# A Fourier mixing layer and an MLP mixer on one core: a rebuilt kernel with 64x64 array tiles, resident filters and no output transposes

## The chip, the cores and the metric

One core of a Trainium2 chip. The time is the device time of one execution in microseconds (us). Runs of the undisturbed state are called "fast". A "ratio" is always the mean time of one kernel's fast runs over that of the kernel before in the same rounds, so it is not quite the ratio of the medians that stand beside it. The profile is one traced execution; its span is about 2 us shorter than the measured time.

Names of engines: PE is TensorE's matmuls, PEld its weight loads, DVE is VectorE, ACT ScalarE, POOL GpSimd, SP SyncE. A *group* or *block* below is 512 tokens of the MLP. A *pair* is two of the eight batches; both kernels work on four pairs. PSUM is where the matmuls leave their sums; an *eviction* is the copy of a PSUM tile into a tile that later steps read.

## The reference, cut to what matters

```python
def _attn_ref(x, filt_r, filt_i):                 # x: (8, 3136, 256)
    X = np.fft.rfft(x, axis=1)
    Y = X * (filt_r + 1j * filt_i)[None]          # one filter per frequency and channel
    return np.fft.irfft(Y, n=x.shape[1], axis=1)

def _moe_ref(x, U, V, w_ch1, w_ch2):              # U: (3136, 32), V: (32, 3136)
    xt = x.transpose(0, 2, 1)
    h = xt @ U @ V                                # low-rank mixing over the sequence
    u = x + h.transpose(0, 2, 1)
    ch = np.maximum(u @ w_ch1, 0.0) @ w_ch2       # 256 -> 1024 -> 256
    return u + ch
```

Both kernels take the length 3136 = 64 x 49 apart: a transform over 64 (first stage), a store and a reload that turn the data, a transform over 49 with the filter and its inverse (here called *mid*), a store and a reload, and the inverse transform over 64 (last stage). Then the low-rank term, then the MLP. Everything between is float16, sums are float32.

## The kernel before: the parts that the argument touches

```python
    def stage_f1c(bp):          # first stage: 64 rows, 128 columns (real and imaginary of 64 frequencies)
        ...
                    nc.tensor.matmul(pf1[:, 0:nn * DM], w64c[64 * i:64 * i + 64, :],
                                     x16[64 * i:64 * i + 64, n2 * DM:(n2 + nn) * DM], ...)
    def stage_mid(bp):          # per frequency: two matmuls, two multiplies, two matmuls, ACT copy
        ...                     # filters come again for each pair: fag, fbg
    def stage_i2(bp):           # last stage: 66 rows, 64 columns, writes y16
        ...
    def stage_lr(bp):           # low rank, after the whole of y16 is there
        for r in range(N2):     # 49
            for i in range(2):
                nc.tensor.matmul(ph1[i][32 * i:32 * i + 32, :],           # 64 rows, 32 columns
                                 usb[64 * i:64 * i + 64, r * RANK:(r + 1) * RANK],
                                 y16[64 * i:64 * i + 64, r * DM:(r + 1) * DM], ...)
        ...
        for r in range(N2):
            pg = ppf.tile([128, DM], F32, tag="m", bufs=3)
            for i in range(2):
                nc.tensor.matmul(pg[64 * i:64 * i + 64, :],               # 32 rows, 64 columns
                                 vsb[32 * i:32 * i + 32, r * N1:(r + 1) * N1],
                                 h1sb[32 * i:32 * i + 32, :], start=True, stop=True)
            nc.vector.tensor_add(y16[:, r * DM:(r + 1) * DM], y16[:, r * DM:(r + 1) * DM], pg[:, :])
    def stage_mlp(bp):
        def mm2_part(prev):
            ...
            for eh in range(2):
                pc = ppf.tile([128, 512], F32, tag="m", bufs=3)
                for t in range(8):
                    nc.tensor.matmul(pc[:, 0:nr * 128],                   # weights stationary
                                     w2sb[:, t * DM + eh * 128:t * DM + eh * 128 + 128],
                                     h16[t][:, 0:nr * 128], start=(t == 0), stop=(t == 7))
                cht = sb.tile([128, 512], F16, tag="cht", bufs=2)
                nc.scalar.copy(cht[:, 0:nr * 128], pc[:, 0:nr * 128])
                for rr in range(nr):                                      # back to tokens in rows
                    nc.tensor.transpose(pq[:, rr * DM + eh * 128:rr * DM + eh * 128 + 128],
                                        cht[:, rr * 128:(rr + 1) * 128], idn[:, 0:128])
        ...
```

The stages are Python generators, woven together: while one pair is in its last stage, low rank and MLP, the next pair is in mid and the one after that in its first stage.

Of the kernel before, what the change touches and what calls it, by code (L numbers as in the profile page):

```python
# [12 lines left out]


SEQ = 3136
N1, N2 = 64, 49
NK1 = 33
DM = 256
RANK = 32  # L20
NF = SEQ // 2 + 1
NG = [3] * 11
NGP = 7


def _consts():
    W64 = np.exp(-2j * np.pi * np.outer(np.arange(N1), np.arange(N1)) / N1)
    W49 = np.exp(-2j * np.pi * np.outer(np.arange(N2), np.arange(N2)) / N2)
    tw = np.exp(-2j * np.pi * np.outer(np.arange(N1), np.arange(N2)) / SEQ)
    w64c = np.concatenate([W64.real.T, W64.imag.T], axis=1)  # L30
    perm = np.arange(N2)
    perm[25:] = 73 - perm[25:]
    tc1 = np.zeros((NK1, N2, 98))
    tc2 = np.zeros((NK1, N2, 98))
    for a in range(NK1):
        Wp = W49 * tw[a][None, :]
        tc1[a, :, :N2] = Wp.real.T[:, perm]
        tc1[a, :, N2:] = Wp.imag.T[:, perm]
        tc2[a, :, :N2] = -Wp.imag.T[:, perm]
        tc2[a, :, N2:] = Wp.real.T[:, perm]  # L40
    ctw = np.exp(2j * np.pi * np.outer(np.arange(NK1), np.arange(N2)) / SEQ)
    g1 = np.zeros((NK1, 98, 98))
    g2 = np.zeros((NK1, 98, 98))
    for a in range(NK1):
        T1 = (W49.conj() * ctw[a][:, None]) / SEQ
        tr, ti = T1.real.T[perm, :], T1.imag.T[perm, :]
        g1[a][:N2, :N2] = tr
        g1[a][:N2, N2:] = ti
        g1[a][N2:, :N2] = -tr
        g1[a][N2:, N2:] = -ti  # L50
        g2[a][:N2, :N2] = -ti
        g2[a][:N2, N2:] = tr
        g2[a][N2:, :N2] = -ti
        g2[a][N2:, N2:] = tr
    g1[:, 49 + 25:98, :] *= -1.0
    g2[:, 25:49, :] *= -1.0
    w = np.exp(2j * np.pi * np.outer(np.arange(N1), np.arange(NK1)) / N1)
    cr = w.real.copy()
    ci = -w.imag.copy()
    cr[:, 1:32] *= 2.0  # L60
    ci[:, 1:32] *= 2.0
    s2 = np.zeros((66, 64))
    s2[0::2, :] = cr.T
    s2[1::2, :] = ci.T
    f16 = np.float16
    return (w64c.astype(f16), tc1.astype(f16), tc2.astype(f16),
            g1.astype(f16), g2.astype(f16), s2.astype(f16))
# [3 lines left out]
def kernel(  # L71
# [12 lines left out]
    B = x.shape[0]  # L84
    npair = B // 2
    w64_np, tc1_np, tc2_np, g1_np, g2_np, s2_np = _consts()

    w64_d = nc.inline_tensor(np.ascontiguousarray(w64_np), name="w64c")
    tcc_d = nc.inline_tensor(np.ascontiguousarray(
        np.stack([tc1_np, tc2_np], 1).reshape(NK1 * 2, N2, 98)), name="tcc")  # L90
    g12_d = nc.inline_tensor(np.ascontiguousarray(
        np.stack([g1_np, g2_np], 1).reshape(NK1 * 2, 98, 98)), name="g12")
    s2_d = nc.inline_tensor(np.ascontiguousarray(s2_np), name="s2")

    ct1 = nc.dram_tensor("ct1", (B, NK1, N2, 2, DM), F16, kind="Internal")
    ct2 = nc.dram_tensor("ct2", (B, N2, NK1, 2, DM), F16, kind="Internal")

    cst = ctx.enter_context(tc.tile_pool(name="cst", bufs=1))
    sb = ctx.enter_context(tc.tile_pool(name="sb", bufs=1))
    ppf = ctx.enter_context(tc.tile_pool(name="ppf", bufs=2, space=bass.MemoryType.PSUM))  # L100

    ftd = nc.dram_tensor("ftd", (2, 98, NK1, DM), F16, kind="Internal")
    ftdv = ftd.ap()
    for t, part, src in ((0, 0, filt_r), (0, 49, filt_i), (1, 0, filt_i), (1, 49, filt_r)):
        nc.gpsimd.dma_start(
            ftdv[t, part:part + 25],
            bass.AP(tensor=src.tensor, offset=0,
                    ap=[[64 * DM, 25], [DM, NK1], [1, DM]]))
        nc.gpsimd.dma_start(
            ftdv[t, part + 25:part + 49],  # L110
            bass.AP(tensor=src.tensor, offset=64 * DM,
                    ap=[[64 * DM, 24], [-DM, NK1], [1, DM]]))

    w64c = cst.tile([128, 128], F16)
    nc.sync.dma_start(w64c[0:64, :], w64_d.ap())
    nc.sync.dma_start(w64c[64:128, :], w64_d.ap())
    tcc = cst.tile([N2, NK1 * 2 * 98], F16)
    nc.sync.dma_start(tcc, tcc_d.ap().rearrange("a n m -> n a m"))
    g12 = cst.tile([98, NK1 * 2 * 98], F16)
    nc.sync.dma_start(g12, g12_d.ap().rearrange("a j m -> j a m"))  # L120
    s2t = cst.tile([66, 64], F16)
    nc.sync.dma_start(s2t, s2_d.ap())
    idn = cst.tile([128, 128], F16)
    make_identity(nc, idn)
# [4 lines left out]
    usb = cst.tile([128, N2 * RANK], F16)  # L129
    uap = moe_U.rearrange("(q r) p -> q r p", q=N1)  # L130
    nc.gpsimd.dma_start(usb[0:64, :], uap)
    nc.gpsimd.dma_start(usb[64:128, :], uap)
    vsb = cst.tile([64, N2 * N1], F16)
    vnat = sb.tile([RANK, SEQ], F32, tag="x16")
    nc.sync.dma_start(vnat, moe_V)
    nc.vector.tensor_copy(vsb[0:32, :], vnat.rearrange("p (q r) -> p r q", q=N1))  # L136
    nc.sync.dma_start(vsb[32:64, :], vsb[0:32, :])

    st = [dict() for _ in range(npair)]

    def stage_x(bp):
        x16 = sb.tile([128, N2 * DM], F16, tag="x16")
        st[bp]["x16"] = x16
        for i, b in enumerate((2 * bp, 2 * bp + 1)):
            nc.gpsimd.dma_start(x16[64 * i:64 * i + 64, :],
                                x[b].rearrange("(q r) d -> q (r d)", q=N1))

    def stage_f1c(bp):
        bA, bB = 2 * bp, 2 * bp + 1
        x16 = st[bp]["x16"]  # L150
        ne = [0]
        for g0 in range(0, N2, NGP):
            gn = min(NGP, N2 - g0)
            asbg = sb.tile([128, 2 * NGP * DM], F16, tag="asbg", bufs=2)
            for i in range(2):
                for n2 in range(g0, g0 + gn, 2):
                    nn = min(2, g0 + gn - n2)
                    pf1 = ppf.tile([128, 512], F32, tag="a", bufs=3)
                    nc.tensor.matmul(pf1[:, 0:nn * DM],  # L159
                                     w64c[64 * i:64 * i + 64, :],  # L160
                                     x16[64 * i:64 * i + 64, n2 * DM:(n2 + nn) * DM],
                                     start=True, stop=True)
                    dst = asbg[:, (i * NGP + n2 - g0) * DM:(i * NGP + n2 - g0 + nn) * DM]
                    if ne[0] % 2:
                        nc.scalar.copy(dst, pf1[:, 0:nn * DM])  # L165
                    else:
                        nc.vector.tensor_copy(dst, pf1[:, 0:nn * DM])
                    ne[0] += 1
            for i, b in enumerate((bA, bB)):
                for c in range(2):  # L170
                    nc.gpsimd.dma_start(  # L171
                        ct1.ap()[b, :, g0:g0 + gn, c, :],
                        asbg[64 * c:64 * c + NK1,
                             i * NGP * DM:(i * NGP + gn) * DM].rearrange(
                                 "k (n d) -> k n d", d=DM))
            yield

    def load_a2g(bp, gi):
        kgn = NG[gi]
        kg0 = sum(NG[:gi])  # L180
        a2g = sb.tile([N2, 2 * NG[0] * 2 * DM], F16, tag="a2g", bufs=2)
        for i, b in enumerate((2 * bp, 2 * bp + 1)):
            nc.sync.dma_start(
                a2g[:, i * NG[0] * 512:i * NG[0] * 512 + kgn * 512],
                ct1.ap()[b, kg0:kg0 + kgn].rearrange("k n c d -> n k (c d)"))
        return a2g

    def load_ftab(kg0, kgn):
        fag = sb.tile([98, kgn * DM], F16, tag="fag", bufs=2)
        fbg = sb.tile([98, kgn * DM], F16, tag="fbg", bufs=2)  # L190
        nc.sync.dma_start(fag.rearrange("p (k d) -> p k d", k=kgn),
                          ftdv[0, :, kg0:kg0 + kgn, :])
        nc.sync.dma_start(fbg.rearrange("p (k d) -> p k d", k=kgn),
                          ftdv[1, :, kg0:kg0 + kgn, :])
        return fag, fbg

    def stage_mid(bp):
        bA, bB = 2 * bp, 2 * bp + 1
        a2g_next, ft_next = st[bp].pop("pre", None) or (load_a2g(bp, 0), load_ftab(0, NG[0]))
        pend = []  # L200
        done_groups = []

        def do_i1(items):
            for (k1, kl, uv, esb) in items:
                pi1 = ppf.tile([128, 512], F32, tag="q", bufs=2)
                for l in range(2):
                    nc.tensor.matmul(pi1[0:98, :],  # L207
# [5 lines left out]
        for gi in range(len(NG)):  # L213
# [27 lines left out]
            if len(pend) > 1:  # L241
                do_i1(pend.pop(0))
# [26 lines left out]
    def stage_i2(bp):  # L269
# [4 lines left out]
        for cl in range(0, N2 * DM, 1024):  # L274
# [20 lines left out]
            if nchip % 3 == 0:  # L295
                yield
# [186 lines left out]
```

## Time and profile before

| | before |
|---|---|
| median of the first 3 runs | 1033.84 us (1032.45 to 1037.25) |
| span of the profile | 1029.0 us |
| PE, DVE, ACT busy | 857, 499, 397 us |
| time at half clock | about 455 us (0 to 353, 500 to 551, 712 to 746, 879 to 896) |
| 512 tokens in the stretch with the MLP alone | 9.8 us |

From the page of the kernel before: span and busy times, the lines of part 2 for PE and its granted clock (40 equal slices, tenths), and the chain that ended last (share by engine, then by engine, tile and line).

```profile
span 1029.0 us, 11955 instructions
...
PE 857.2 (83%) x4184; PEld 338.0 (33%) x4184; DVE 498.5 (48%) x833; ACT 396.8 (39%) x769; POOL 278.7 (27%) x418
...
PE   0017098786999999999999999998999988988884
PEclk9999999999999999999757999998599999699997
...
PE 66%; ACT 6%; DMA 4%; DVE 3%; POOL 2%; issue 2%; ACTq 0%; POOLq 0%; SPq 0%; DVEq 0%
PE pc L337 17%; PE phh L376 16%; PE py L287 4%; PE pg L317 3%; PE pq L344 3%; ACT cht L342 3%; PE pt L362 2%; DMA ct<-esb 2%; DMA x_972<-in_x_dram 1%; POOL ct L256 1%; PE ph_1252 L304 1%; ACT asbg L165 1%; ACT esb L211 1%; DVE y_3234 L321 1%; DVE y_5483 L321 1%
```

The chain is two thirds PE, and well over half of that share are the matmuls of the MLP (L337, L376), the input transposes (L362) and the output transposes (L344). The clock line shows three dips (at some 500 to 550, 720 to 745 and 875 to 900 us), a fourth in the last slice, where the program ends, and otherwise nines. That line is treacherous here: the clock records of this trace begin at 353 us, and where nothing is recorded a 9 is printed.

From the timeline of the kernel before (start, duration, engine, line, operation; "x2" are merged neighbours, and a merged duration runs from the first start to the last end):

```profile
start us, us, engine line op out<-in xcount [idle before <-releaser]
439.70 0.38 PE L337 MATMUL pc<-h_5_2726,w2sb 128*128 128x512 f16 x1
439.92 0.38 PE L337 MATMUL pc<-h_6_2727,w2sb 128*128 128x512 f16 x1
...
522.26 0.66 PE L207 MATMUL pi_4017<-uv,g_77 98*98 98x512 f16 x1 [0.18 <-DVE uv L237]
522.86 1.08 PE L230 MATMUL pf_3999<-a2g,tcc 49*98 49x512 f16 x2
...
900.79 0.38 PE L337 MATMUL pc<-h_7_7994,w2sb 128*128 128x512 f16 x1
901.85 0.40 PE L344 MATMUL pq<-idn,cht 128*128 128x128 f16 x4 [0.68 <-ACT cht L342]
902.08 0.38 PE L337 MATMUL pc<-h_0_7987,w2sb 128*128 128x512 f16 x1
```

At 439 us 512-wide matmuls start 216 ns apart. At 523 us one takes 0.66 us and two take 1.08 us together, so they start some 430 ns apart: half the rate. Up to 353 us, too, 512-wide matmuls that follow each other start 380 to 460 ns apart, most of them 427 or more, and none near 216 (but for pairs that run at once on two tiles). So the clock is halved for the first 353 us also. The last three lines are one block's round trip: the second MLP matmul is issued for the last time at 900.79, the transposes of its output come 1.06 us later (0.68 us of it PE sits idle, released by the ACT copy).

### The profile page before, as it was taken

Reading aid. Unit: us, or ns where it says so; the run is one execution under the profiler, and the core shown is the slowest. Engines: PE = TensorE matmul, PEld = TensorE weight load, DVE = VectorE, ACT = ScalarE, POOL = GpSimd, SP = SyncE. Lnnn points to the kernel's source line nnn. Section 1 sums busy time; section 2 is a strip of 40 time slices with the busy share of each in tenths; the row PEclk is TensorE's granted clock in tenths of the full one; section 3 lists DMA queues with packets and bytes.
Section 4 is the critical chain, followed back from the end, with each engine's and each line's share of the span. In section 5 each row is a group of like instructions: output and inputs, shape, how many; then the busy total and the mean of one; then the engine's idle time right before and its main releaser. Section 6 shows DMA issues by size and latency. Waiting matters only on the chain.

```text
span 1029.0 us, 11955 instructions
## 1 busy us (share of the span) xinstructions
PE 857.2 (83%) x4184; PEld 338.0 (33%) x4184; DVE 498.5 (48%) x833; ACT 396.8 (39%) x769; POOL 278.7 (27%) x418
## 2 busy tenths in 40 slices
PE   0017098786999999999999999998999988988884
PEld 0001022221233344344433444454344434434332
DVE  0026066552357575546675754566744332733322
ACT  0004042232221356666114555652265543245442
POOL 3006044634223254214323420245210111001101
PEclk9999999999999999999757999998599999699997
DMA  9763744674328355433323554354143212012121
GB/s 164 124 154 111 158 131 131 165 202 137 99 71 199 102 166 157 126 92 96 109 76 113 156 174 121 82 141 151 36 114 107 64 43 66 1 41 62 49 55 47
DMA packets 93501, 113.07 MB, mean 110 GB/s; under 512 B 27092, under 2 KB 78716, under 8 KB 92796
## 3 DMA queue, kind: packets, MB, share of 16 engines
q0 software_dynamic: 32960, 70.00, 27.8%
q1 hardware_dynamic: 60480, 42.30, 14.4%
q8 instruction: 33, 0.54, 0.2%
q14 instruction: 28, 0.23, 0.1%
HBM read 77.30 MB, written 55.49 MB: 129 GB/s over the span
## 4 chain that ended last, share of the span: by engine, by line
PE 66%; ACT 6%; DMA 4%; DVE 3%; POOL 2%; issue 2%; ACTq 0%; POOLq 0%; SPq 0%; DVEq 0%
PE pc L337 17%; PE phh L376 16%; PE py L287 4%; PE pg L317 3%; PE pq L344 3%; ACT cht L342 3%; PE pt L362 2%; DMA ct<-esb 2%; DMA x_972<-in_x_dram 1%; POOL ct L256 1%; PE ph_1252 L304 1%; ACT asbg L165 1%; ACT esb L211 1%; DVE y_3234 L321 1%; DVE y_5483 L321 1%
## 5 line engine op out<-in xcount | busy, mean ns | idle before, releaser
L256 POOL DMA_DIRECT2D ct<-esb x160 | 119.3, 750 | 177.4 <-ACT esb L211 166.3
L350 POOL DMA_DIRECT2D out_dram<-och x104 | 56.3, 546 | 347.7 <-DVE och L347 325.3
L171 POOL DMA_DIRECT2D ct<-asbg x112 | 77.9, 699 | 160.8 <-ACT asbg L165 146.9
L342 ACT CAST cht<-pc 128x512 f16<-128x512 f32 (+1 forms) x104 | 58.3, 561 | 148.6 <-PE pc L337 148.6
L376 PEld LDWEIGHTS <-w1sb 128*128 128x128 f16 x832 | 76.1, 100 | 105.0 <-issue 42.3
L337 PEld LDWEIGHTS <-w2sb 128*128 128x128 f16 x832 | 76.7, 98 | 75.8 <-issue 4.4
L159 PEld LDWEIGHTS <-w64c 64*128 64x128 f16 x224 | 19.5, 108 | 148.1 <-issue 135.9
L317 PE MATMUL pg<-h1sb,vsb 32*64 32x256 f16 x392 | 64.2, 387 | 1.9 <-ACT h1sb L312 0.3
L230 PEld LDWEIGHTS <-tcc 49*98 49x98 f16 x264 | 32.5, 154 | 92.0 <-issue 88.3
L207 PEld LDWEIGHTS <-g_77 98*98 98x98 f16 x264 | 33.5, 151 | 73.0 <-issue 61.9
L344 PE MATMUL pq<-idn,cht 128*128 128x128 f16 x392 | 39.9, 222 | 20.5 <-ACT cht L342 19.4
L159 PE MATMUL pf_102<-x_98,w64c 64*128 64x512 f16 x1 | 0.6, 582 | 67.0 <-DMA x_98<-in_x_dram 67.0
L344 PEld LDWEIGHTS <-cht 128*128 128x128 f16 x392 | 23.1, 97 | 58.4 <-ACT cht L342 56.6
L317 PEld LDWEIGHTS <-vsb 32*64 32x64 f16 x392 | 25.9, 126 | 49.5 <-issue 47.4
L136 DVE CAST vsb<-vnat 32x3136 f16<-32x3136 f32 x1 | 5.7, 5697 | 50.2 <-DMA vnat<-in_moe_V_dram 50.2
L287 PEld LDWEIGHTS <-s2t 66*64 66x64 f16 x200 | 12.3, 113 | 46.9 <-issue 46.0
L165 ACT CAST asbg<-pf_105 128x512 f16<-128x512 f32 x1 | 0.6, 585 | 66.0 <-PE pf_105 L159 66.0
L304 PEld LDWEIGHTS <-usb 64*32 64x32 f16 x392 | 19.2, 96 | 19.6 <-issue 16.1
L293 DVE CAST y_982<-py 128x512 f16<-128x512 f32 (+1 forms) x13 | 8.2, 665 | 33.1 <-PE py L287 33.1
L321 DVE TENSOR_TENSOR y_982<-y_982,pg 128x256 f16<-128x256 f16 x49 | 17.3, 413 | 11.2 <-PE pg L317 11.2
L321 DVE TENSOR_TENSOR y_5483<-y_5483,pg 128x256 f16<-128x256 f16 x49 | 17.1, 412 | 10.1 <-PE pg L317 10.1
L230 PE MATMUL pf_322<-a2g,tcc 49*98 49x512 f16 x2 | 1.1, 628 | 24.6 <-DMA a2g<-ct 24.6
(2306 smaller groups left out, 2054.6 us busy)
## 6 DMA issues: line engine op xcount, KB each, us to landing
out_dram<-och POOLq DMA_DIRECT2D x96, 256.0 KB, 3.7
ct<-asbg POOLq DMA_DIRECT2D x112, 115.5 KB, 2.7
a2g<-ct SPq DMA_DIRECT2D x88, 147.0 KB
ct<-esb POOLq DMA_DIRECT2D x176, 73.5 KB, 3.4
fag<-ftd SPq DMA_DIRECT2D x44, 147.0 KB
fbg<-ftd SPq DMA_DIRECT2D x44, 147.0 KB
x_98<-in_x_dram POOLq DMA_DIRECT2D x2, 1568.0 KB, 14.6
x_311<-in_x_dram POOLq DMA_DIRECT2D x2, 1568.0 KB, 17.5
```

Source lines behind the costliest of these rows:

```text
L171: nc.gpsimd.dma_start(ct1.ap()[b, :, g0:g0 + gn, c, :], asbg[64 * c:64 * c + NK1, i * NGP * DM:(i * NGP + gn) * DM].rearrange("k (n d) -> ...
L207: nc.tensor.matmul(pi1[0:98, :], g12[:, (k1 * 2 + l) * 98:(k1 * 2 + l + 1) * 98], uv[:, l * 512:(l + 1) * 512], start=(l == 0), stop=(l == 1))
L230: nc.tensor.matmul(pf2[0:98, :], tcc[:, (k1 * 2 + l) * 98:(k1 * 2 + l + 1) * 98], rhs, start=(l == 0), stop=(l == 1))
L256: nc.gpsimd.dma_start(ct2.ap()[b, :, kh0:kh0 + khn, c, :], src)
L287: nc.tensor.matmul(py[64 * i:64 * i + 64, 0:w], s2t[:, :], e2c[i][:, sub:sub + w], start=True, stop=True, tile_position=(0, 64 * i))
L317: nc.tensor.matmul(pg[64 * i:64 * i + 64, :], vsb[32 * i:32 * i + 32, r * N1:(r + 1) * N1], h1sb[32 * i:32 * i + 32, :], start=True, stop= ...
L321: nc.vector.tensor_add(y16[:, r * DM:(r + 1) * DM], y16[:, r * DM:(r + 1) * DM], pg[:, :])
L337: nc.tensor.matmul(pc[:, 0:nr * 128], w2sb[:, t * DM + eh * 128:t * DM + eh * 128 + 128], h16[t][:, 0:nr * 128], start=(t == 0), stop=(t = ...
L342: nc.scalar.copy(cht[:, 0:nr * 128], pc[:, 0:nr * 128])
L344: nc.tensor.transpose(pq[:, rr * DM + eh * 128:rr * DM + eh * 128 + 128], cht[:, rr * 128:(rr + 1) * 128], idn[:, 0:128])
L350: nc.gpsimd.dma_start(out[b].rearrange("(q r) d -> q r d", q=N1)[:, r0:r0 + nr, :], och[64 * i:64 * i + 64, 0:nr * DM])
L376: nc.tensor.matmul(phh[:, 0:nr * 128], w1sb[:, dh * 1024 + t * 128:dh * 1024 + (t + 1) * 128], ut[dh][:, 0:nr * 128], start=(dh == 0), sto ...
```

## The change: its intent, and its core

The kernel was rewritten. Its intents were: smaller array tiles where operands have 64 rows and 64 columns, so that four matmuls run at once; the filter table read once and kept; the low-rank product U computed on the spectrum (before the last FFT stage) and V accumulated into the PSUM tile of that stage, so that neither a separate pass nor an addition is left; the MLP's second matmul with the hidden tokens as stationary operand, so that its output has tokens in its rows and needs no transpose; and the last FFT stage done per group of 512 tokens, just ahead of the MLP that uses it. The diff is almost the whole file; its core, with cuts marked "...":

```diff
 # first FFT stage
-    w64c: [128, 128], one 64-row tile, 128 output columns, 56 matmuls per pair
+    wf1: [128, 64]; 48 matmuls per pair on 64x64 tiles, four at once
+                for i in range(nb):
+                    for h in range(2):
+                        nc.tensor.matmul(pf[64 * h:64 * h + 64, i, :],
+                            wf1[64 * i:64 * i + 64, :],
+                            u.x[c][64 * i:64 * i + 64, h, 2 * half:2 * half + 2, :], ...)
 # mid: filters resident, one matmul instead of two, one multiply instead of two
-        fag, fbg = load_ftab(...)                # again for each pair
+    fab = cst.tile([98, NK, 2, DM], F16)         # once
+            pz = ps.tile([128, 512], F32, tag="z", bufs=2, name="pz")
+            nc.tensor.matmul(pz[0:98, 0:bd], tf2[:, k * 98:(k + 1) * 98],
+                             a2[slot // 4][:, slot % 4, :], start=True, stop=True)
+            nc.vector.tensor_mul(uv..., zin, fin)            # 98 x 1024
+            # do_i1: pe = ps.tile(tag="z", bufs=2); two matmuls; nc.scalar.copy(esb, pe)
 # low rank
-    def stage_lr(bp): 98 + 98 matmuls, 49 additions
+    def low_rank(u):                             # U on the spectrum: 25 matmuls
+            nc.tensor.matmul(ph[32 * g:32 * g + 32, 0:bd], ut2[:, rp * RANK:(rp + 1) * RANK],
+                             u.e2[j // cj][:, s, j % cj, :], ...)
+    def stage4(gr):                              # last FFT stage of one group, then V on top
+                nc.tensor.matmul(pu[64 * s:64 * s + 64, h, :], s2[64 * h:64 * h + 64, :],
+                                 e2[64 * h:64 * h + 64, s, j % cj:j % cj + jc, :],
+                                 start=True, stop=False, ...)
+                nc.tensor.matmul(pu[:, h, jj * bd:(jj + 1) * bd], vsb[:, v0:v0 + 128], u.h1,
+                                 start=False, stop=True, ...)
 # MLP
+    mm1(gr, t): two matmuls, then nc.scalar.activation(h, ph, RELU)   # all on ACT, two PSUM banks
-                cht copy, 8 transposes, one addition of 1024
+            nc.tensor.matmul(gr.pc[:, col * DM:(col + 1) * DM],
+                             gr.h[tt][:, i * 128:(i + 1) * 128],      # hidden tokens stationary
+                             w2sb[:, tt * DM:(tt + 1) * DM], ...)
+            nc.vector.tensor_add(dst, gv, uv)
```

The rest is a fixed plan: eight steps per group, in each of which stand two first-matmuls of this group and four second-matmuls of the group before. Over the 104 steps of a pair, 34 steps of the next pair's mid and 13 of the first stage of the pair after that are spread.

## The prediction

> **What bounds the kernel now.** TensorE: the page gives PE 857 of 1029 us; the chain of waits is 66% PE, led by the two MLP matmuls (17% and 16%). DVE, ACT and DMA are half busy or less. Three losses sit in that time.
>
> - Half clock. The clock records show 0.50 at 500-551, 712-746, 879-896 us; before 353 us nothing is recorded, but the timeline shows 512-wide matmuls 427 ns apart there, against 216 ns later. So about 450 us run at half rate, in stages of 32- to 98-row matmuls; dense 128-row MLP work ends each (the Trainium skill, "TensorE: Matmul & The Clock Gate", Part 1, says activity releases the throttle; this trace agrees).
> - Low-rank stages without MLP in them: some 55 us per pair when cold.
> - MLP waits. In the MLP-only end the timeline shows 9.8 us per 512 tokens; its 32 matmuls at 216 ns and 16 transposes at 56 ns need 7.8 us. The rest is mostly the matmul-copy-transpose round trip.
>
> **What the change does per pair of batches (PE, full clock; estimates from those intervals).**
> - First FFT stage: 56 64-row matmuls become 48 64x64 ones, four at once (column pairs start 3 ns apart in this trace): per four 0.22 us plus 0.22 us for two tile-mode switches: 6 us.
> - Mid: 132 matmuls become 99: 21 us.
> - Low rank: 98+98 narrow matmuls and 49 adds vanish. U on the spectrum: 2 us. V accumulates in PSUM with the last FFT stage: 0.9 us per group.
> - MLP: 98 output transposes and their copies go. First matmul 16x216 ns; second 32 of 256 columns, 109 ns each, as weight loads already hide behind 56 ns transposes; 8 input transposes 0.45 us. Group: 7.4+0.9 us.
> - Sum: 131 us with both FFT stages of later pairs woven in, 125 for the third pair, 102 for the last: 489 us if nothing waits. ACT (8.4 per 11.2 us; all ReLUs there, 0.59 us each) and DVE (7.9 us) stay below, but ReLU has two PSUM buffers, shared with the transposes: I add 8%: 530 us, at full clock.
>
> **The front.** The instruction order puts the first intermediate store behind all filter, V and MLP-weight loads on the gpsimd queue (before, such loads took 38 us; x of one pair 19 us), and the eviction buffer is, until U is read, single. I expect that store to land at 70 us, pair 0's first stage done at 105 us, mid from 110 us. Mid alone is a loop of matmul, 98x1024 multiply (1.24 us, estimated from 693 ns at 512), next matmul: 2.0 us cold, 33 times, plus evictions: 73 us. Then store, 3.2 MB reload, low rank: dense MLP from about 200 us (before: 345 us). Tail 4 us.
>
> **Prediction: 725 us, range 670 to 790.** Faster by over 2%: 0.98; within 2%: 0.01; slower: 0.01.
>
> **Signs.** Right if: 427 ns spacing ends near 200 us and the clock stays 1.0; PE over 90% busy after; a 512-token group takes 8.5-9.5 us in the last pair, 11-12.5 us in the first two; four 64x64 matmuls start within 10 ns; mid alone steps at 2 us with DVE its releaser; pair 0's first-stage evictions wait for DMA.
>
> **What would make it wrong.** 64x64 tiles of different rows not overlapping (+0.65 us per group, +30 to 60 us); two ReLU buffers or in-order ACT stalling PE more; the reload before low rank stalling PE in every pair (+5 us each); stores blocked behind x loads; or a shorter front: down to 670.

## More of the kernel before

From the windows of the kernel before (busy time of each engine in a stretch, number of instructions, granted clock, DMA share):

```profile
core 0: us, PE busy (x) PEld busy (x) DVE busy (x) ACT busy (x) POOL busy (x), PEclk, DMA share, GB/s
353.00:500.00 147.00, 145.91 (x874) 64.16 (x872) 85.87 (x128) 85.46 (x171) 52.16 (x78) 1.00 0.44 124
500.00:551.00 51.00, 50.23 (x170) 15.47 (x169) 35.33 (x81) 10.84 (x19) 12.48 (x17) 0.50 0.29 89
```

Between 500 and 551 us PE is busy for 50.2 of 51 us and yet runs at half clock. This stretch is the low-rank stage of the second pair with the mid stage of the third woven in, and at its end the first MLP matmuls of the second pair. So it is not idle PE that holds the clock down here.

## The result, and the profile after

| | before | after |
|---|---|---|
| median | 1033.14 us (1030.56 to 1037.25, 4 runs) | 719.12 us (718.99 to 720.15, 4 runs) |
| ratio of fast runs | | 0.6964, 95% interval 0.6944 to 0.6983 |
| span of the profile | 1029.0 us | 716.9 us |
| PE, DVE, ACT busy | 857, 499, 397 us | 581, 288, 384 us |
| first MLP matmul | 334 us | 217 us |
| half clock | about 455 us | about 218 us |
| 512 tokens, MLP alone | 9.8 us | 8.31 us (now with last FFT stage and V) |
| bytes moved by DMA | 113 MB | 98 MB |

From the page of the changed kernel, the same lines as before:

```profile
span 716.9 us, 9884 instructions
...
PE 581.4 (81%) x3797; PEld 330.4 (46%) x3797; DVE 288.1 (40%) x311; ACT 383.7 (54%) x634; POOL 126.8 (18%) x197
...
PE   0000126766789999998999999999999999999996
PEclk9999999999999999999999999999999999999999
...
PE 70%; DMA 13%; ACT 6%; issue 5%; POOL 2%; DVE 2%; SPq 1%; ACTq 0%; DVEq 0%; POOLq 0%
PE phh L379 22%; PE pc L415 21%; PE pe L257 10%; PE pz L279 5%; DMA ct_0<-asb 3%; PE pu L356 3%; PE pt L371 3%; ACT esb L266 3%; DMA x_75<-in_x_dram 3%; PE pu L350 2%; DMA fab<-in_filt_r_dram 2%; PE pf L214 2%; DMA e_2022<-ct_1 2%; ACT asb L222 2%; DMA fab<-in_filt_i_dram 2%
```

From its windows, columns as above: the front up to the reload (two stretches), the three pairs with work woven in, and the last pair.

```profile
0.00:108.00 108.00, 12.00 (x71) 2.98 (x71) 10.90 (x11) 16.19 (x14) 40.32 (x68) 1.00 0.97 155
108.00:212.00 104.00, 76.07 (x201) 26.96 (x197) 60.10 (x50) 30.02 (x48) 30.52 (x46) 1.00 0.75 184
217.00:607.00 390.00, 386.12 (x2742) 232.03 (x2742) 187.90 (x208) 264.93 (x452) 55.97 (x83) 1.00 0.52 138
607.00:717.00 110.00, 102.71 (x766) 66.54 (x764) 25.86 (x39) 69.13 (x116) 0.00 (x0) 0.99 0.27 74
```

Once the MLP has begun, PE is busy 99% of the time at full clock, up to its last matmul at 710 us. Before that, in 212 us, it is busy for 88 us, all at half clock: the 1.00 printed in the first two rows is again the missing record, and the two `pe` matmuls of 512 columns in the timeline below take 1.06 us together. The kernel is now two kernels: a front bound by waits, and a rest bound by TensorE.

From its timeline in the last pair, one step and a half of a group:

```profile
640.41 0.41 PE L350 MATMUL pu<-e_5380,s_91 64*64 64x512 f16 x4
640.75 0.60 PE L356 MATMUL pu<-h_5575,vsb 128*128 128x512 f16 x2
641.19 0.27 PE L415 MATMUL pc<-w2sb,h_6103 128*128 128x256 f16 x1
641.30 0.27 PE L415 MATMUL pc<-w2sb,h_6124 128*128 128x256 f16 x1
641.41 0.27 PE L415 MATMUL pc<-w2sb,h_6133 128*128 128x256 f16 x1
...
641.63 0.59 PE L379 MATMUL phh<-ut,w1sb 128*128 128x512 f16 x2
```

The four 64x64 matmuls (L350, 512 wide) take 0.41 us together, as long as one. The second MLP matmuls (L415) start 109 ns apart, although each brings its own 128-column weights. Nothing in brackets: PE waits for nothing.

From its timeline in the front, where mid runs alone, and from its waits (engine and line that waited, for whom: us in total, times, longest):

```profile
166.69 0.58 ACT L266 CAST esb<-pe 98x512 f16<-98x512 f32 x1 [1.57 <-PE pe L257]
167.33 0.58 PE L279 MATMUL pz<-a_437,tf_87 98*98 98x512 f16 x1 [0.72 <-ACT esb L266]
167.71 1.06 PE L257 MATMUL pe<-uv,g_89 98*98 98x512 f16 x2
167.95 1.22 DVE L286 TENSOR_TENSOR uv<-pz,fab 98x1024 f16<-98x1024 f32 x1 [0.93 <-PE pz L279]
168.80 0.58 ACT L266 CAST esb<-pe 98x512 f16<-98x512 f32 x1 [1.52 <-PE pe L257]
```

```profile
engine line waited for: us in total, times, longest us
DVE asb L224 <- DMA ct_0<-asb: 72.0, 5, 42.9
PE pz L279 <- ACT esb L266: 20.3, 32, 0.7
```

One mid step is 2.11 to 2.16 us. It is a ring: matmul `pz`, two matmuls `pe`, the ACT copy of `pe`, and then the next `pz`, which the brackets show released by that copy (0.67 to 0.72 us idle).

### The profile page after: what moved, and what is told of

Same layout as the page of the kernel before. It is cut to its first block, busy times and chain, and to the rows that moved or that the text cites. A ratio compares the mean times of both kernels' runs of the same rounds, so it can differ in the third digit from the quotient of the medians.

```text
span 716.9 us, 9884 instructions
## 1 busy us (share of the span) xinstructions
PE 581.4 (81%) x3797; PEld 330.4 (46%) x3797; DVE 288.1 (40%) x311; ACT 383.7 (54%) x634; POOL 126.8 (18%) x197
## 4 chain that ended last, share of the span: by engine, by line
PE 70%; DMA 13%; ACT 6%; issue 5%; POOL 2%; DVE 2%; SPq 1%; ACTq 0%; DVEq 0%; POOLq 0%
PE phh L379 22%; PE pc L415 21%; PE pe L257 10%; PE pz L279 5%; DMA ct_0<-asb 3%; PE pu L356 3%; PE pt L371 3%; ACT esb L266 3%; DMA x_75<-in_x_dram 3%; PE pu L350 2%; DMA fab<-in_filt_r_dram 2%; PE pf L214 2%; DMA e_2022<-ct_1 2%; ACT asb L222 2%; DMA fab<-in_filt_i_dram 2%
## 5 line engine op out<-in xcount | busy, mean ns | idle before, releaser
L379 PE MATMUL phh<-ut,w1sb 128*128 128x512 f16 (+1 forms) x832 | 237.6, 367 | 1.4 <-ACT h_2242 L382 0.2
L286 DVE TENSOR_TENSOR uv<-pz,fab 98x1024 f16<-98x1024 f32 x132 | 160.8, 1222 | 91.5 <-PE pz L279 91.2
L266 ACT CAST esb<-pe 98x512 f16<-98x512 f32 x128 | 74.6, 586 | 104.3 <-PE pe L257 103.3
L257 PE MATMUL pe<-uv,g_89 98*98 98x512 f16 x264 | 98.0, 462 | 3.0 <-DVE uv L286 2.0
L224 DVE CAST asb<-pf 128x1024 f16<-128x1024 f32 x24 | 29.3, 1222 | 97.0 <-DMA ct_0<-asb 72.0
L257 PEld LDWEIGHTS <-g_89 98*98 98x98 f16 x264 | 37.2, 144 | 54.3 <-issue 45.6
L222 ACT CAST asb<-pf 128x1024 f16<-128x1024 f32 x24 | 24.3, 1013 | 62.2 <-PE pf L214 60.5
L373 DVE COPY ut<-pt 128x1024 f16<-128x1024 f16 (+1 forms) x52 | 34.2, 657 | 15.2 <-PE pt L371 12.7
L279 PEld LDWEIGHTS <-tf_87 98*98 98x98 f16 x132 | 19.6, 148 | 17.3 <-issue 15.4
L268 POOL DMA_DIRECT2D ct_3<-esb x16 | 11.4, 710 | 90.2 <-ACT esb L266 83.6
L268 POOL DMA_DIRECT2D ct_1<-esb x16 | 11.5, 721 | 74.6 <-ACT esb L266 69.0
L268 POOL DMA_DIRECT2D ct_2<-esb x16 | 11.5, 720 | 63.5 <-ACT esb L266 50.4
L268 POOL DMA_DIRECT2D ct_0<-esb x16 | 11.9, 744 | 39.1 <-ACT esb L266 39.1
L350 PEld LDWEIGHTS <-s_91 64*64 64x64 f16 x192 | 6.5, 103 | 19.4 <-issue 18.8
L227 POOL DMA_DIRECT2D ct_3<-asb x12 | 7.7, 648 | 27.2 <-ACT asb L222 27.2
L227 POOL DMA_DIRECT2D ct_1<-asb x12 | 7.6, 640 | 12.5 <-ACT asb L222 12.5
```

The lines of the kernel that those rows point to most:

```text
L222: nc.scalar.copy(dst, src)
L224: nc.vector.tensor_copy(dst, src)
L257: nc.tensor.matmul(pe[0:98, 0:bd], g3[:, (2 * k + l) * 98:(2 * k + l + 1) * 98], uv[:, l * bd:(l + 1) * bd], start=(k != 32 and l == 0), s ...
L266: nc.scalar.copy(st["esb"][:, slot % 2, :], pe[0:98, 0:bd])
L268: nc.gpsimd.dma_start(dram(u.ct2, (slot - 1) * 98 * bd, [[bd, 98], [98 * bd, 2], [1, bd]]), st["esb"])
L279: nc.tensor.matmul(pz[0:98, 0:bd], tf2[:, k * 98:(k + 1) * 98], a2[slot // 4][:, slot % 4, :], start=True, stop=True)
```

## The experiments

There were twelve, in four submissions: the first three; then `a_nolr`, `a_k128`, `a_z` and `a_front`; then `b_burst`, `a_fs`, `a_frontz` and `a_fzs`; last `a_act`. The `b_` kernels change the kernel before, the `a_` kernels the changed one ("after").

| run | what | median us | ratio to before |
|---|---|---|---|
| b_swap | before + MLP output without transposes | 1007.93 | 0.9659 |
| b_nolr | before without low rank (wrong result) | 904.44 | 0.8767 |
| b_warm | before + useless matmuls in mid and V | 1153.98 | 1.1174 |
| b_burst | before + short bursts of useless matmuls | 1038.20 | 1.0042 |
| a_nolr | after without low rank (wrong result) | 684.73 | 0.6619 |
| a_k128 | after, 64-row tiles padded to 128 rows | 738.38 | 0.7150 |
| a_fs | after, filters loaded again for each pair | 727.53 | 0.7044 |
| a_act | after, 2 of 8 ReLUs done twice | 725.09 | 0.7023 |
| a_z | after, own PSUM banks in the first pair's mid | 698.98 | 0.6782 |
| a_front | after, first stage issued ahead of the loads | 701.19 | 0.6795 |
| a_frontz | both | 684.17 | 0.6619 |
| a_fzs | both, and stores on another queue | 679.16 | 0.6573 |

### b_swap: one part of the change alone

```diff
-                cht copy and transposes, weights stationary
+                    for t in range(8):
+                        nc.tensor.matmul(pc[:, rr * DM:(rr + 1) * DM],
+                                         h16[t][:, (p0 + rr) * 128:(p0 + rr + 1) * 128],
+                                         w2sb[:, t * DM:(t + 1) * DM], start=(t == 0), stop=(t == 7))
```

> The kernel before with one part of the change alone: the second MLP matmul takes the hidden tokens as the stationary operand (256 columns of weights moving), so its output needs no copy and no transpose. Theory 'round trip' (the 2 us per 512-token block beyond 7.8 us are the waits for the copy between matmul and transpose): per block about 0.84 + 0.5 us of waits and 8 x 56 ns of transposes go, about 1.7 us x 49 blocks = 85 us, so about 950 us, and a block in the MLP-only end takes about 8 us instead of 9.8. Rival 'covered' (in the mixed stages other work fills these waits): only the transposes' 22 us and the waits of the last pair go, about 1000 us.

Measured: 1007.93 us (993.4 to 1019.64; the two fast runs took 993.4 and 1000.38, and the ratio of 0.9659 is theirs). From its timeline in the MLP-only end:

```profile
961.72 0.61 PE L358 MATMUL pt<-idn,y 128*128 128x128 f16 x8
962.30 3.65 PE L338 MATMUL pc<-w2sb,h 128*128 128x256 f16 x32
965.79 4.01 PE L372 MATMUL phh<-ut,w1sb 128*128 128x512 f16 x16
969.65 0.55 PE L358 MATMUL pt<-idn,y 128*128 128x128 f16 x7
```

With the MLP alone the mechanism is what the round-trip theory said: a block takes 7.9 us instead of 9.8, without a wait. In the stretches with other stages woven in most blocks take 8.2 us instead of 10 or more, and the 48 steps from one block to the next within the pairs shrank by 87 us together. Not all of that is waits, for work left the blocks too. The whole gained 35 by the ratio, 30 in the profiled run. Most of the rest, 65 us, was given back: the time from the start of a pair's last block to the start of the next pair's first grew from 50, 57 and 30 us to 82, 88 and 33. The traces show what fills these gaps. In the first of them TensorE ran 13 first-stage and no last-stage matmuls before, and 52 and 32 with the shorter MLP (and 43 of mid in both). In the kernel before the others had stood among the MLP's matmuls, and partly in the waits: there, in the third pair, a block with 8 last-stage matmuls in it took 9.85 us and one with none 9.83. The Python order of the generators is the same in both; the order that the framework's scheduler makes of it now puts them together with the low-rank work, and there they run at half clock (0.5 in 470 to 490, 497 to 562 and 709 to 763 us, before in 500 to 551 and 712 to 746). Of the 65 us, some 26 are the work moved there (estimated from its columns at 216 ns per 512), and the half clock, which after its first end lasts 157 us instead of 102 in the records up to the last pair's MLP, costs some 27 more (half of the difference). So the waits were real, and were partly covered: the fast runs' 997 us are close to the rival's 1000. What neither theory had is that the shorter MLP pushed narrow work into the slow stretch.

### b_nolr and a_nolr: the price of the low-rank part, before and after

```diff
-        gb = chain(stage_i2(bp), stage_lr(bp), stage_mlp(bp))      # b_nolr
+        gb = chain(stage_i2(bp), stage_mlp(bp))
-    low_rank(...); the V matmuls in stage4                         # a_nolr
```

> The kernel before without its low-rank stage (wrong result on purpose): what that stage costs there. Theory 'narrow and cold': its 392 + 392 matmuls of 32 or 64 rows and 196 adds stretch over some 45 us per pair, mostly at half clock and with little else in them: about 120 us less, about 910 us. Rival 'only its work': its matmuls at full clock and pairwise overlap are some 16 us per pair, 65 us in all: about 970 us.

> The changed kernel without its low-rank part (wrong result on purpose): neither U on the spectrum nor the V matmuls that accumulate behind the last FFT stage. Theory 'cheap': per group two 512-wide matmuls at 216 ns go, per pair the 25 U matmuls (about 2 us) and some front work: 4 x (12.25 x 0.43 + 2) + 3 us, about 32 us less, about 687 us. Rival 'hidden' (the matmuls fill waits of the ReLU buffers): less than 10 us, about 712 us. In the kernel before the same removal took away 127 us.

Measured: 904.44 us without it in the kernel before (128 us less), 684.73 us in the changed one (34 us less). Their outputs are wrong, which doesn't matter for the times. The first agrees with "narrow and cold" (910 expected), the second with "cheap" (687 expected). The low-rank part costs 94 us less than it did: this is the largest single piece of the gain that a run separates. In b_nolr the full clock comes at 294 us instead of 353, and its later falls last 3 to 7 us each instead of 17 to 51: without the stretch of narrow matmuls the clock stays up.

### b_warm and b_burst: what lifts the clock

```diff
+        for _ in range(count):                     # into the tile that the real matmul overwrites
+            nc.tensor.matmul(o[:, 0:n], w1sb[:, 0:128], w1sb[:, 0:n], start=True, stop=True)
 # b_warm: 2 of 512 columns ahead of each mid pair, 1 of 256 ahead of each V pair
 # b_burst: 24 of 512 columns once in the first pair's last stage, 48 of 256 once in each V stage
```

> The kernel before with useless full-array matmuls added (128 rows, 128 columns; two of 512 columns ahead of each of the 132 second-stage matmul pairs, one of 256 columns ahead of each of the 196 V pairs, written into the same PSUM tile and overwritten). Theory 'array use' (the clock is halved while the matmuls fill only part of the 128x128 array, even if they follow each other without gaps): the 512-wide matmuls of those stages come 216 ns apart instead of 427 in most of the stretches from 130 to 345, 500 to 550 and 712 to 746 us, and the time falls in spite of the added work, by 50 to 120 us: about 950 us. Rival 'gaps' (the clock falls because of idle gaps or because the stage waits for DMA): the clock stays halved, and the added 264 x 0.43 + 196 x 0.21 us makes it slower: about 1100 us.

Measured: 1153.98 us, ratio 1.1174. A miss. The clock stayed halved up to 399 us, although a third of TensorE's work in these stretches was now on the full array. By its own text this speaks for the rival, but PE had no gaps there either. From the windows of its kept trace (the run of 1165.01 us), a stretch at half clock:

```profile
559.40:641.40 82.00, 81.51 (x246) 23.57 (x245) 39.46 (x80) 10.83 (x19) 14.51 (x20) 0.50 0.19 58
```

So a number was worked out for each of the 43 rises and 43 falls of the clock that the 14 traces record: in the 3.41 us before it, the sum over matmuls of columns x (rows used / 128) x the time of a column (216 or 427 ns per 512), divided by 3.41 us; column tiles on the same rows at the same time count once. Before every rise this *row share* was 0.72 or more; before every fall 0.39 or less; without a rise it reached at most 0.82 in a window, without a fall it went down to 0.38. (A second working of the same sum, with the overlaps counted a little otherwise, gave 0.76, 0.38, 0.78 and 0.38: the edges are good to some 0.04, and at each the two cases just overlap.) In between the clock stays as it is. b_warm's dose mostly stayed below 0.7. The next run put the same kind of work into bursts that fill one such window.

> The kernel before with short dense bursts of useless full-array matmuls: 24 of 512 columns once, in the last FFT stage of the first pair, and 48 of 256 columns once in each pair's V stage (about 5 us of full-clock work, 10 us at half clock, each). Theory 'share of the rows' (computed from the traces so far: the clock doubles after 3.4 us in which the streamed rows are over about 0.7 of 128 rows x time, and halves when they are under about 0.4): each burst is followed by 512-wide matmuls 216 ns apart or a clock of 1.0 in the records, from the first burst at about 245 us on; in the V stages the clock falls back within about 10 us. The time changes little, 1000 to 1060 us. Rival 'only the MLP lifts it' (length of the busy stretch, or TensorE's stationary operands of 128 rows in the stage itself): the clock stays halved up to the MLP as before, and the time grows by about 40 us.

Measured: 1038.20 us, ratio 1.0042, as expected. From its timeline, at the first burst (L271):

```profile
247.45 7.31 PE L271 MATMUL py<-w1sb 128*128 128x512 f16 x24
254.69 0.62 PE L293 MATMUL py<-e2c,s2t 66*64 66x512 f16 x4
```

Its clock records rise to 1.0 at 251.5 us, inside the burst: 24 matmuls of 512 columns took 7.31 us, between the 5.2 us of full and the 10.2 us of half clock. Four 66-row matmuls right after it take 0.62 us; one alone took 0.58 us at 245 us. The clock then stays up for 31 us in the last stage and U (row share mostly 0.4 to 0.5), where without the burst it was halved, and falls at 282 us. In the four V stages each burst raises the clock (295.8, 500.6, 715.7, 882.9) and it falls 6.8 to 6.9 us later, where the row share is 0.3 or less. So one dense burst lifts the clock, and narrow matmuls lose it. Whether rows or cells of the array are what counts is not settled: two rises (b_swap at 490, b_warm at 996 us) came in U stages with 0.3 of the cells but over 0.9 of the rows in use, which speaks for rows. That is computed, not varied by itself.

### a_k128: 64x64 tiles undone by half

```diff
-    wf1[64 * i:64 * i + 64, :], u.x[c][64 * i:64 * i + 64, h, ...]     # 64 rows
+    wf1[:, 64 * i:64 * i + 64], u.x[c][:, h, ...]                      # 128 rows, half of them zero weights
 # the same for s2 in the last stage
```

> The changed kernel with its 64x64 tiles undone by half: the first and the last FFT stage contract over all 128 rows, with weights padded by 64 rows of zeros, so that two instead of four matmuls run at once (column pairs only). The result is the same. Theory 'PE is the bound after the front': each of the 48 groups and of the 25 first-stage chunks that are woven in costs 0.22 us more, 48 x 0.22 + 25 x 0.22 = 16 us, about 735 us; no effect in the front, where these stages wait for DMA. Rival 'clock' (rows of the array in use hold the clock up): no loss or a gain in the front.

Measured: 738.38 us, 19 us more than after (expected 16). A group in the last pair takes 8.52 instead of 8.31 us: 0.21 us per visit of the narrow tiles, one 512-wide matmul. Only 13 of the 20 us by which the profile grew lie after the first MLP matmul, where 16 were expected; 7 lie in the front (MLP from 224.2 instead of 217.0 us), where none was expected: mid steps with a first-stage visit in them took up to 3.73 instead of 2.89 us there, at half clock. The row half of the 64x64 tiling is worth all this together, under 3%; it is not where 314 us came from.

### a_fs: filters not resident

```diff
+    nc.sync.dma_start(ftd.ap(), fab...)                                 # once
+        if u.n: nc.sync.dma_start(fab[:, k0:k0 + kn, :, :], ftd...)     # again for pairs 1 to 3
```

> The changed kernel with its filters not resident: the table is written to memory once and loaded again for each of the three later pairs, 27 loads, 9.9 MB in all, over the same place (results the same). Theory 'residency saves only traffic': after the front TensorE is 97 to 100% busy and the DMA engines half busy, so 10% more bytes cost nothing there: 718 to 724 us, some us in the front at most, where the table is stored. Rival 'traffic counts': 9.9 MB at the 137 GB/s that the page shows on average is 70 us; even a fifth of it would show as 14 us.

Measured: 727.53 us, 8 us more than after; above the range of the first theory and below the rival's. Where the 8 us lie is plain in the windows. The MLP began 11 us later, at 228.2 us, so the same stretch of work is compared shifted by some 10 us, first a_fs, then after:

```profile
350.00:600.00 250.00, 249.16 (x1761) 151.82 (x1758) 133.22 (x144) 171.98 (x295) 32.29 (x47) 1.00 0.53 149
```

```profile
340.00:590.00 250.00, 249.15 (x1761) 151.79 (x1760) 133.21 (x144) 171.79 (x295) 32.31 (x47) 1.00 0.50 137
```

The same 1761 matmuls, the same busy times within 0.2 us, at 149 instead of 137 GB/s. Residency is worth nothing once TensorE is the bound. The 11 us are the front's, where the table's 3.3 MB had to be stored beside everything else.

### a_act: why two ReLU banks did not make TensorE wait

```diff
         nc.scalar.activation(h[:, 0:n], ph[:, 0:n], RELU)
+        if t % 4 == 1:
+            nc.scalar.activation(h[:, 0:n], ph[:, 0:n], RELU)
```

> The changed kernel with two of the eight ReLUs of each group done twice, on the same PSUM tile into the same output (results the same): 104 more ACT instructions of 0.59 us, each holding one of the two ReLU banks twice as long. The prediction had added 8% to the woven part for waits at these two banks; the trace shows under 2%. Theory 'slack' (between a ReLU's matmul and the next use of its bank stand two steps of other TensorE work, 1.7 us at least, and ACT is 68% busy): a group in the last pair still takes 8.3 us, the whole 719 to 724 us. Rival 'on the edge' (the waits are absent by a narrow margin): most of the added 0.59 us comes through, up to 61 us; from 735 us on this would hold.

Measured over five rounds: 725.09 us, 6 us more, a miss of the expected range by 1 us at its upper end. A group of the last pair takes 8.44 us: of the 1.2 us added per group to ACT 0.13 us come through. From the windows, a_act and then after:

```profile
600.00:700.00 100.00, 99.50 (x735) 62.46 (x729) 24.10 (x37) 77.62 (x135) 0.00 (x0) 1.00 0.24 66
```

```profile
600.00:700.00 100.00, 99.80 (x743) 64.04 (x742) 24.45 (x36) 67.19 (x113) 0.00 (x0) 1.00 0.24 65
```

ACT goes from 67 to 78% busy, PE from 99.8 to 99.5%. There is slack, though it isn't unlimited.

### a_z, a_front, a_frontz, a_fzs: what bounds the front

```diff
-            pz = ps.tile([128, 512], F32, tag="z", bufs=2, name="pz")
+            pz = ps.tile([128, 512], F32, tag="z" if u.n else "o", bufs=2, name="pz")   # a_z
 # a_front: f1(units[0]) stands ahead of the loads of fab, usb, vnat, w1sb, w2sb; usb in another buffer
-                nc.gpsimd.dma_start(dram(u.ct2, ...), st["esb"])
+                (nc.gpsimd if u.n else nc.sync).dma_start(dram(u.ct2, ...), st["esb"])  # a_fzs
```

> The changed kernel, with the first matmul of the intermediate stage of the first pair put into the PSUM banks that are idle until the MLP begins; two banks for it, two for the third matmul, instead of one each. Theory 'one bank each': while this stage runs alone a step of 2.14 us is matmul, two matmuls, ACT copy of 0.59 us, next matmul in the freed bank, in a ring; with the ring cut a step takes as long as its longest engine, 3 x 427 ns or the 1.22 us multiply, about 1.35 us, so 33 x 0.75 us = 25 us less, about 694 us. Rival 'DVE loop' (the ring is matmul, multiply, matmul as predicted): the same 25 us, but then the multiply, not the copy, ended the wait in the trace. Rival 'DMA' (the step waits for loads or stores): under 5 us.

Measured: 698.98 us, 20 us less than after. Timeline of its first pair's mid:

```profile
143.04 0.38 PE L279 MATMUL pz<-a,tf 98*98 98x512 f16 x1
143.25 0.59 PE L257 MATMUL pe<-uv,g 98*98 98x512 f16 x2
143.88 0.59 ACT L266 CAST esb<-pe 98x512 f16<-98x512 f32 x1 [0.50 <-PE pe L257]
144.17 0.38 PE L279 MATMUL pz<-a,tf 98*98 98x512 f16 x1 [0.32 <-DVE uv L286]
```

A step now takes 1.13 us at full clock and 1.28 us at half clock (3 x 427 ns), and `pz` is released by the multiply instead of the copy. The 32 steps took 40 us instead of 69, and the MLP began 28 us earlier, at 189 us. The first theory holds, the predicted ring through DVE does not. The clock even rose by itself at 117 and 134 us, where three 98-row matmuls followed each other without gaps. Of the 28 us, 20 came through: work of the next pair that the longer ring had let in during the front (16 of its 33 mid steps before the first MLP matmul, here 4) was left to the woven part, where the first pair took 133 us instead of 128, and the reload before the low-rank matmuls now makes PE wait:

```profile
PE pu L350 <- DMA e<-ct: 12.3, 1, 12.3
```

In the changed kernel PE spent that time on the next pair's mid.

> The changed kernel with its first FFT stage issued ahead of the loads of filters, U, V and MLP weights, and U in another buffer, so that the eviction buffer is double from the start. Theory 'queue order' (the first stage of pair 0 waits from about 20 to 105 us for its store, which stands behind those loads in one queue): the first stage ends at about 40 us, the filters land at about 70 us and the intermediate stage begins there instead of at 108 us: about 35 us less, about 684 us. Rival 'DMA volume' (the first 100 us are bound by the bytes to be moved, whatever their order): the second pair's x and its first stage come later by as much and hold up the front's end; under 10 us.

Measured: 701.19 us, 18 us less, half of the expected 35. The first mid matmul came at 58 us instead of 111, the next only at 78, when the filters had landed. But mid then took until 160 us (before 180). One line of its waits between 92 and 170 us:

```profile
POOL x L132 <- PE pf L165: 13.6, 1, 13.6
```

POOL stood for 13.6 us before one x load whose buffer was not free; the stores of mid stand behind it in program order, their three buffers were full, so ACT and with it PE stood too. That is one of the risks that the prediction named, found in the variant rather than in the change. The two parts of this edit, the order and the second eviction buffer, were not tried apart.

> Both front changes together: first FFT stage issued ahead of the other loads, and separate banks for the first and third matmul of the first pair's intermediate stage. Alone they gave about 20 and 18 us. Theory 'separate waits': they add, about 681 us. Rival 'shared limit' (in the reordered front the gpsimd queue stands still behind one x load that waits for the second pair's first stage, and the stores of the intermediate stage stand behind it): the bank change gains less here than alone, about 690 us.

Measured: 684.17 us. By the ratio the two gains, 0.0182 and 0.0169, add to 0.0351, and 0.0345 was measured: they add. "Separate waits" is confirmed, the rival is not.

> As the kernel with both front changes, and the stores of the first pair's intermediate stage issued from the sync engine instead of gpsimd, so that they don't stand behind x loads. Theory 'head of the queue': in the reordered front the gpsimd engine waited 13.6 us for one x load's buffer while three filled store buffers waited behind it, and the copy engine and TensorE behind those; without this, 8 to 13 us less than with the two front changes. Rival 'DMA volume': the bytes in the front are the limit by now; within 3 us of the kernel with the two front changes.

Measured: 679.16 us, 5 us less than a_frontz: between the two theories' numbers. The queue was part of it: in the trace of a_frontz one mid step takes 17.0 us, here none after the filters have landed takes over 6.4. POOL still waits 23 us for an x load, which no longer blocks a store of this mid. This is the fastest version: ratio 0.6573 to before, 40 us under the change. What then bounds its front (the MLP begins at 171 us) was not taken further.

## Why the prediction was right, point by point

**The total** was predicted as 725 us and measured as 719.12, inside 670 to 790. It is a sum in which errors cancelled, so that it came within 1% is luck, and the text's own terms (200 for the front, 530 for the woven part, 4 for the tail) add up to 734, not 725. Measured in the profile: 217 us to the first MLP matmul, and 500 us from there to the end.

**The woven part: the mis-sized term.** The work was sized well: 131, 131, 125 and 102 us for the four pairs against 127.6, 134.0, 128.7 and 109.6 us (the last with a tail of 7 us after the last matmul). The first of these is flattered: 16 of the next pair's mid steps had run in the front, 10 us of the 131 by an estimate of three matmuls of 216 ns each. The sizes came from intervals in the trace of before: 216 ns, 56 ns, 309 and 336 ns at a change of tile mode. The Trainium skill, "TensorEngine Tiling (Array Packing)", section Key Properties, says that a change of tiling mode drains TensorE, without a figure; the traces show 309 ns going in and 332 coming out instead of 216, so 0.21 us per visit. The step that failed is the 8% "for waits" at two PSUM banks for the ReLU: 41 us were added, about 11 measured as all that exceeds 489, or some 21, 7 of them tail, if those 10 us are counted too. Between two uses of a ReLU bank stand two steps of other TensorE work, of 1.04 us each in the last pair (8.31 us for eight), against 0.59 us for a ReLU, and ACT was 68% busy, not 75%; a_act shows that this leaves slack.

**The front: undersized.** Dense MLP was predicted from 200 us and began at 217. The parts: first store landed at 61 us (predicted 70), first stage stored at 105.6 (105), mid's first matmul at 111 (110), mid's last one at 183.5 (183; its last `pz` at 180). So the parts agree, and what was too small is what follows mid: the last stores, the 3.2 MB reload and the low-rank matmuls took until 217, not 200. The prediction had nothing else running there; the trace shows the 16 mid steps of the next pair there, at half clock up to 212.7 us, and no wait of PE for the reload.

**The ring in mid** was right in length (2.0 against 2.11 to 2.16 us) for a wrong reason. The prediction said matmul, multiply, matmul, with DVE the releaser. The trace shows ACT's copy, and a_z shows that the ring closes over the two shared PSUM banks.

**Half clock.** Predicted: it ends near 200 us and the clock stays at 1.0. The record rises at 212.7 us and falls at 714.4, after the last matmuls. Right. The prediction gave as reason the skill's "TensorE: Matmul & The Clock Gate", Part 1, where activity releases the throttle. The records show two levels only, 0.5 and 1.0, as the page says, and stretches between changes that are multiples of 3.41 us (51.2 is 15 of them), which agrees with the page's 3413 ns window. What counts as activity is told more finely by b_burst than by the page.

**Smaller signs.** Four 64x64 matmuls started 3 ns apart (within 10 predicted); the skill's "TensorE: Matmul & The Clock Gate", Part 3, gives about 4 ns, and this agrees. PE over 90% busy after the front: 99%. A group in the last pair: 8.31 us, below the predicted 8.5 to 9.5, by the same missing waits. In the first two pairs half of the groups took 10.7 to 11.6 us and most of the others less, so many lay below the predicted 11 to 12.5. First-stage evictions of pair 0 waited for DMA: 72.0 us in five waits.

**Where 314 us came from.** Two parts were separated by runs. The low-rank part costs 34 us instead of 128. The round trip of the MLP output cost 1.9 us in a block with the MLP alone; its removal by itself gave 35 us in all, because other work had partly filled these waits, and ran at half clock once it was pushed out of them. These overlap with the loss of the half clock itself, which fell from 455 to 218 us of the span, so the three are not to be added. The row half of the 64x64 tiling gave about 19 us, resident filters about 8, all of it in the front. The rest (a quarter fewer mid matmuls, fewer and longer evictions, a better-filled front) was not separated.

## What to carry to other kernels

Read the spacing of equal matmuls before believing the clock line, and keep work that uses few rows of the array woven into dense work: pooled by itself it runs at half clock, and a speed-up elsewhere can push it there. When several stages share TensorE, find the engine that is full and sum measured intervals; waits at a shared buffer should be added only where the time between two uses is shorter than the ring through it. In a front with little to overlap, look at which wait closes each ring (a PSUM bank, the order in one DMA queue): two such changes were worth 35 us here, more than the new tiling and the resident filters together.

## What the Trainium skill lacked or had wrong

- "TensorE: Matmul & The Clock Gate", "HAM oscillation", puts the half clock down to idle gaps of TensorE of over about 3.4 us. Here it was halved from 500 to 551 us with PE busy 50.2 of 51 us, on matmuls that nearly all had 32 to 98 rows. Computed from 14 traces, it rose only after 3.41 us with a row share of at least 0.72 and fell only after one of at most 0.39.
- The same page, "Back-to-back issue gap", gives about 131 ns (512 columns) and 81 ns (128 columns) per matmul for a sustained stream in a real kernel. The traces of before and after show 216 and 56 ns at full clock, each with its own weight load, which is the page's formula for a single isolated gap.
- The same page, Part 3, lists weight loads as overlapping with running matmuls only when the row group differs, although its text above that list also names a background weight buffer. Here 128-row weights, 98 ns each, were loaded behind 128-row matmuls of 256 columns that followed each other after 109 ns.
- "TensorEngine Tiling (Array Packing)", Key Properties, has no figure for a change of tiling mode: 309 ns going in and 332 ns coming out (after), instead of 216.
